# Block 0's partial sums in a fused FNet + MLP layer: residual x copied to DRAM first, block 0 added to it by DMA, and part of the PSUM reads moved from VectorE to ScalarE

## The chip, the cores and the metric

One core of a Trainium2 chip runs the whole layer. The core has TensorE (PE, matrix products into PSUM; its weight loads are listed as PEld), VectorE (DVE), ScalarE (ACT), GpSimd (POOL) and SyncE (SP). SP and POOL also issue DMAs: SP's appear in the profile as queue q1 (hardware_dynamic) and POOL's as q0 (software_dynamic). An adding DMA (`accum_op=ALU.add`) adds its source to what lies at its destination; in this kernel they are all issued by POOL.

The metric is the device time in microseconds of one execution. The kernel before took 1277.23 us, the median of three runs (1274.8 to 1278.28).

## What is computed

With x of 2048 x 576, normalized by rows to xn, the reference is

```python
x = A_x
xn = _layernorm(x, axis=-1)
# A: Real(DFT_seq(DFT_hidden(xn)))
a = jnp.einsum("bsd,ed->bse", xn, dft_hid_re)
b = jnp.einsum("bsd,ed->bse", xn, dft_hid_im)
A = jnp.einsum("ts,bse->bte", dft_seq_re, a) - jnp.einsum("ts,bse->bte", dft_seq_im, b)
# B: an MLP with a hidden width of 4608
h = jnp.maximum(jnp.einsum("bsd,df->bsf", xn, w1), 0)
B = jnp.einsum("bsf,fd->bsd", h, w2)
return x + A + B
```

All inputs are float32. The kernel splits each operand into a float16 high and a float16 low part, and takes three float16 products for one.

## The kernel before

**Stages.** The MLP comes first (up to about 940 us), then the two DFT stages. The MLP's hidden width of 4608 is cut into 9 blocks b of 512 columns, and the 2048 rows of x into 4 groups g of 512 rows (4 tiles of 128). The loop over `steps` (L888) runs over b outside and g inside. A step computes the first product of (b, g) (`mlp1_step` and others, L310 and L335; from b = 2 on `pair_products`, L440), turns it into hidden values h (`mlp1_out`, L343 to L361), and weaves in the second product of the step before, `mlp2` (L496).

**The second product.** `mlp2(b, g, n)` for n = 0 to 6 is one of seven products of a Strassen-like scheme for the four quarters (row, col) of the group's 512 x 576 result. Each is 24 matmuls of 288 columns (L510) into a PSUM tile of the pool `ps2`, which has only two buffers. Products 0, 2, 4 and 6 accumulate in one place, each read out in turn; product 1 has a place of its own, and products 3 and 5 share a third. PE may add the next product to a place only when the one before has been read. The same two buffers are lent to the transposes of x (`transposes`, L254, tiles named pt) and to small products that find a maximum (`power_pe`, L152, tiles named pm).

**Reading a product out.** For b > 0, products 0, 2, 3 and 6 are the first for their quarter: ACT copies them, scaled, into a small buffer (L519). Products 1, 4 and 5 are added to that buffer by DVE (L521), and products 1, 4, 5 and 6 complete a quarter, which POOL then adds to DRAM (`spill`, L523). For b = 0 all seven are added by DVE (L521) into `accs[g]`, the SBUF tile that holds the group's rows of x; after product 6 SP writes the four quarters of `accs[g]` to `spill` by plain DMAs (L527). So `spill` starts as x plus block 0's result, and the other blocks are added to it. At the end of the kernel `load_out` (L1102) reads it back.

**What follows in the place of x.** Once a group's quarters have been written out, `accs[g]` is used again: `sums_x` (L391) forms sums of the transposed xn in float32 (L405 to L409), and writes their high parts (ACT, L412) and low parts (DVE, L414) into the first 2048 of the 2304 floats per partition of `accs[g]`. They are needed from block 2 on. `sums_x` for all groups runs in small steps (`tq`, L887), and the scheduler spreads these over blocks 0 and 1 where it sees room. L414's first write for group 0 lies over parts of the quarters 00 and 01, and so waits for the DMAs that read them.

**Block 0 also normalizes x.** During step (0, g), the tiles of group g + 1 are normalized: statistics (DVE, L200 to L222; ACT, L210), `normalize` (DVE L242, ACT L243), `remainder` (POOL, L247 and L250; its pair of instructions for tile t is called E(t) below) and `transposes` (PE L258 and L263, called T(t) below; ACT L265 and L268 move the result to SBUF).

**Order.** Each engine works through its instructions strictly in order. The order on each engine is fixed when the kernel is built, by a scheduler that follows the program and moves instructions where it expects an engine to be free. POOL and SP issue their DMAs in order too, and one whose data is not ready holds up what stands behind it.

Of the kernel before, what the change touches and what calls it, by code (L numbers as in the profile page):

```python
# [18 lines left out]
P = 128  # L19
# [10 lines left out]
TG = G // P  # L30
# [4 lines left out]
EH = D // 2  # L35
# [14 lines left out]
def kernel(  # L50
# [17 lines left out]
    nc = tc.nc  # L68
# [17 lines left out]
    accs = [accp.tile([P, TG, D], F32, name=f"acc{g}") for g in range(NG)]  # L86
    acc = [accs[t // TG][:, t % TG] for t in range(NT)]

    spill = {
        (g, row, col): dram.tile([P, TG // 2, EH], F32, name=f"spill{g}_{row}{col}")  # L90
        for g in range(NG) for row in range(2) for col in range(2)
    }
    raws = {}

    def load_x(t):
        nc.sync.dma_start(acc[t], x[t * P : (t + 1) * P, :])
# [321 lines left out]
    def pair_products(b, g, i):  # L418
# [70 lines left out]
    places, sums = {}, {(r, j): None for r in range(2) for j in range(2)}  # L489
    turns = itertools.count()  # L490
    sumbufs = [mlp.tile([P, 2, EH], F32, name="sum0", bufs=1)] + [
        dbuf[:, k : k + 2 * EH].rearrange("p (c e) -> p c e", e=EH)
        for k in (2 * W1B, 2 * W1B + 2 * EH)
    ]

    def mlp2(b, g, n):  # L496

        qa, qb, first, row, col = PRODUCTS[n]
        if first:
            places[n] = ps2.tile([P, 2, 512], F32, tag="ps2", name=f"p2_{b}_{g}_{n}")[:, :, :EH]
        ps = places[PLACE[n]]
        for c in range(2):
            for i in range(NQ):
                h, w = hs[b, g, i], w2s[b, i]
                for j, (x, y) in enumerate(((0, 0), (0, 1), (1, 0))):
                    nc.tensor.matmul(  # L510
                        ps[:, c], h[:, x, qa, c * P : (c + 1) * P], w[:, y, qb],
                        start=first and i == 0 and j == 0, stop=i == NQ - 1 and j == 2,
                        skip_group_check=not first,
                    )
        blocks = accs[g].rearrange("p (h c) (j e) -> p h j c e", h=2, j=2)
        o = sums[row, col] = sums[row, col] if b else blocks[:, row, col]
        if b and n in (0, 2, 3, 6):
            o = sums[row, col] = sumbufs[next(turns) % len(sumbufs)]
            nc.scalar.activation(o, ps, AF.Copy, scale=us[b])  # L519
        else:  # L520
            order["acc"] = nc.vector.scalar_tensor_tensor(o, ps, us[b], o, ALU.mult, ALU.add).ins  # L521
        if b and n not in (0, 2, 3):
            nc.gpsimd.dma_start(spill[g, row, col], o, accum_op=ALU.add)  # L523
        if b == 0 and n == 6:
            for r in range(2):
                for j in range(2):
                    nc.sync.dma_start(spill[g, r, j], blocks[:, r, j])  # L527

    sc, pw, mx = {}, {}, {}

# [180 lines left out]
    load_w2(0, 1)  # L711
    for t in range(2 * TG, NT):
        load_x(t)
    warm = const.tile([P, 1], F32, name="warm")
    nc.scalar.activation(warm, eps, AF.Sqrt)

# [91 lines left out]
    for q in range(7):  # L808
        mlp2(0, 0, q)
# [78 lines left out]
    for n in range(2, len(steps)):  # L888
        b, g = steps[n]
# [28 lines left out]
        if b >= BB:  # L918
            first, second = (pair_products(b, g, i) for i in range(NQ))
            later1, later2 = (lambda q, f=f: f(q, True) for f in (first, second))  # L920
            m = lambda q: mlp2(pb, pg, q)
            end = lambda q: ends and ends.pop(0)()
            ready = lambda q: [work() for _ in range(q)]
            count = lambda q: n > 3 and passes and passes.pop(0)()
            for do, q in (
                (first, P1), (first, P2), (m, 0), (end, 0), (first, P6), (ready, 1),
                (first, P5), (later1, P2), (ready, 1), (m, 1), (end, 0), (second, P1), (ready, 1),
                (first, P7), (m, 2), (second, P2), (ready, 1), (first, P3), (first, P4), (count, 0),
                (later1, P7), (m, 3), (second, P6), (later1, P3), (later1, P4), (later2, P2),
                (ready, 1), (m, 4), (second, P5), (ready, 1), (m, 5), (end, 0), (second, P7),  # L930
                (end, 0), (ready, 1), (m, 6), (count, 0), (ready, 2), (second, P3), (second, P4),
                (later2, P7), (later2, P3), (later2, P4), (ready, 1),
            ):
                do(q)
            for _ in range(4):
                next(tq, None)
            continue
        ps = []
        for i in range(NF):
            if n == 2:  # L940
                ps.append(early.pop(0) if early else mlp1(b, g, i))
            else:
                mlp1_step(b, g, i, ps)
            if i % 2:
                mlp1_out(b, g, i // 2, *ps[i - 1 : i + 1])
            if b == 0 and g + 1 < NG:
                t = (g + 1) * TG + i
                normalize(t)
                remainder(t, nc.gpsimd)
                transposes(t)  # L950
            if n == 2 and i == 2:
                todo += prepare_block(1)
            for _ in range(1 if b else 3):
                work()
            for q in range(2 * i, min(2 * i + 2, 7)):
                mlp2(pb, pg, q)
                if b:
                    next(tq, None)
            if b and i == 3:
                next(tq, None)  # L960
            for _ in range(1 + i % 2 if b else 3):
                work()
            if n > 3 and i % 2 and passes:
                passes.pop(0)()
# [146 lines left out]
    for n, (p, kh) in enumerate(units):  # L1111
# [4 lines left out]
        for i, (q, rq, first, row, col) in enumerate(PRODUCTS):  # L1116
# [6 lines left out]
            for k in range(HK):  # L1123
                r = R[kh * HK + k]
# [6 lines left out]
            o = outs[p][:, row, col * EH : (col + 1) * EH]  # L1131
            nc.vector.scalar_tensor_tensor(o, ps, us["c"][:, n : n + 1], o, ALU.mult, ALU.add)  # L1132
            if kh and i in (2, 4, 5, 6):
                h, j = ((0, 0), (1, 1), (0, 1), (1, 0))[(2, 4, 5, 6).index(i)]
                rows = slice((p + h * NP) * P, (p + h * NP + 1) * P)
                e = slice(j * EH, (j + 1) * EH)
# [55 lines left out]
```

## Time and profile before

| | |
|---|---|
| median of three runs | 1277.23 us |
| the profiled execution, whole time | 1277.31 us |
| its span, first to last instruction | 1275.5 us |
| mean granted TensorE clock | 0.999 |
| PE busy | 97% of the span |
| DVE busy | 78% |
| ACT busy | 57% |
| POOL busy | 12% |

Some 1.8 us of the profiled execution lie outside its span. Block 0's second products, which the change touches, run from about 60 us to about 152 us after the span's start. In the prediction, rows with a start, a duration, an engine and a line come from the timeline (instructions in order of time, runs of equal ones merged); in square brackets stands how long the engine had been idle before, and what released it. A matmul's duration in these rows includes its way through the array, so a row of 12 of them that shows 1.63 us is followed by the next after 1.47 us.

### The profile page before, as it was taken

How to read it: one execution, taken by the hardware profiler on the slowest of the kernel's cores; microseconds unless marked ns; L12 is line 12 of the kernel's file. 1: busy time of each engine (PE TensorE's matmuls, PEld its weight loads, DVE VectorE, ACT ScalarE, POOL GpSimd, SP SyncE). 2: the span in 40 equal slices, each digit the busy share in tenths (PEclk: the TensorE clock that was granted, in tenths of full speed). 3: DMA queues.
4: the chain of work that ended last, by engine and by line, in shares of the span. 5: the costliest groups of instructions: out<-in, count | busy, mean ns of one | idle time of the engine just before them, and what ended most of it. 6: DMA issues, size and time to landing. Idle time of an engine off the chain costs nothing.

```text
span 1275.5 us, 25491 instructions
## 1 busy us (share of the span) xinstructions
PE 1242.4 (97%) x10396; PEld 987.9 (77%) x10396; DVE 998.6 (78%) x1875; ACT 730.1 (57%) x1222; POOL 149.2 (12%) x188
## 2 busy tenths in 40 slices
PE   8799999999999999999999999999999999999998
PEld 7565566888888878888888888877777777777776
DVE  8989997786887777777868877546788788878875
ACT  5846466676677676776766766534553333333332
POOL 2320011111112121211111111200000000000000
PEclk9999999999999999999999999999999999999999
DMA  6112457566766575665666665630043434434320
GB/s 244 43 66 66 133 123 151 131 115 146 143 129 126 134 146 126 128 144 120 121 145 142 132 136 120 122 96 1 1 161 104 146 116 153 129 117 143 121 85 20
DMA packets 60806, 150.75 MB, mean 118 GB/s; under 512 B 6288, under 2 KB 21136, under 8 KB 60688
## 3 DMA queue, kind: packets, MB, share of 16 engines
q1 hardware_dynamic: 42256, 111.36, 26.9%
q0 software_dynamic: 18432, 37.76, 20.9%
q8 instruction: 81, 1.33, 0.4%
q14 instruction: 37, 0.30, 0.1%
HBM read 101.91 MB, written 47.19 MB: 117 GB/s over the span
## 4 chain that ended last, share of the span: by engine, by line
PE 62%; DVE 20%; DMA 8%; ACT 6%; issue 4%; POOL 1%; SPq 0%; ACTq 0%; POOLq 0%; DVEq 0%
PE p L1126 23%; PE bank L440 15%; PE p L510 15%; PE pd L1008 7%; DMA raw_w<-in_w_dram 3%; DVE w2s L183 2%; DMA f<-in_cre_dram 1%; PE p L310 1%; DVE h L448 1%; ACT f L880 1%; DVE h L462 1%; ACT h L459 1%; DVE acc L521 1%; DMA spill<-sums 1%; DVE h L354 1%
## 5 line engine op out<-in xcount | busy, mean ns | idle before, releaser
L510 PE MATMUL p<-w2s,h 128*128 128x288 f16 x3024 | 409.7, 286 | 4.4 <-DVE acc L521 2.1
L510 PEld LDWEIGHTS <-h 128*128 128x128 f16 x3024 | 295.1, 98 | 81.5 <-issue 6.2
L1126 PE MATMUL p<-R,cs 128*128 128x288 f16 x2688 | 329.8, 286 | 1.7 <-DVE o L1132 1.7
L1126 PEld LDWEIGHTS <-cs 128*128 128x128 f16 x2688 | 263.0, 98 | 68.3 <-issue 2.0
L182 ACT ACTIVATE cs<-c,sc_c 128x1024 f16<-128x1024 f32 x112 | 128.4, 1148 | 193.2 <-PE p L1126 145.6
L440 PEld LDWEIGHTS <-w1buf 128*128 128x128 f16 x1600 | 156.5, 98 | 29.1 <-issue 8.1
L183 DVE SCALAR_TENSOR_TENSOR cs<-c,sc_c,cs 128x1024 f16<-128x1024 f32 x112 | 143.6, 1282 | 40.8 <-ACT cs L182 40.7
L440 PEld LDWEIGHTS <-dbuf 128*128 128x128 f16 x1200 | 117.4, 98 | 21.4 <-issue 5.8
L440 PE MATMUL bank<-xT,w1buf 128*128 128x256 f16 x832 | 109.9, 273 | 2.7 <-ACT acc L469 2.6
L462 DVE TENSOR_TENSOR h<-s,h 128x1024 f16<-128x1024 f32 x56 | 68.5, 1223 | 48.8 <-ACT h L459 48.8
L440 PE MATMUL bank<-acc,w1buf 128*128 128x256 f16 x768 | 102.1, 272 | 2.8 <-DVE acc L470 1.5
L1008 PE MATMUL pd<-dbuf,xT 128*128 128x288 f16 x832 | 104.1, 286 | 0.6 <-DVE R L1037 0.6
L1008 PEld LDWEIGHTS <-xT 128*128 128x128 f16 x832 | 80.7, 98 | 22.9 <-issue 2.9
L523 POOL DMA_DIRECT2D spill<-dbuf x74 | 64.3, 871 | 289.8 <-DVE dbuf L521 223.3
L440 PE MATMUL bank<-xT,dbuf 128*128 128x256 f16 x624 | 82.3, 273 | 1.4 <-ACT acc L469 1.4
L447 ACT ACTIVATE h<-acc 128x256 f16<-128x256 f32 x112 | 46.3, 414 | 58.8 <-DVE acc L470 42.5
L440 PE MATMUL bank<-acc,dbuf 128*128 128x256 f16 x576 | 76.6, 272 | 2.5 <-DVE acc L470 1.1
L1132 DVE SCALAR_TENSOR_TENSOR o<-p,us_c,o 128x288 f32<-128x288 f32 x112 | 57.4, 512 | 20.1 <-PE p L1126 19.5
L448 DVE SCALAR_TENSOR_TENSOR h<-acc,h 128x256 f16<-128x256 f32 x112 | 47.2, 421 | 32.0 <-ACT h L447 31.8
L459 ACT ACTIVATE h<-s 128x1024 f16<-128x1024 f32 x56 | 59.0, 1053 | 22.5 <-DVE s L454 21.3
L880 ACT ACTIVATE f<-f 128x1024 f32<-128x1024 f32 x64 | 67.2, 1050 | 5.4 <-DMA f<-in_cre_dram 5.4
L519 ACT ACTIVATE dbuf<-p,c_ub 128x576 f32<-128x576 f32 x74 | 54.2, 732 | 20.5 <-ACT h L447 11.3
(161 smaller groups left out, 1531.5 us busy)
## 6 DMA issues: line engine op xcount, KB each, us to landing
spill<-dbuf POOLq DMA_DIRECT2D x74, 288.0 KB, 5.1
f<-in_cre_dram SPq DMA_DIRECT2D x32, 512.0 KB, 4.3
f<-in_cim_dram SPq DMA_DIRECT2D x32, 512.0 KB, 3.8
c<-in_cre_dram SPq DMA_DIRECT2D x32, 512.0 KB, 4.5
c<-in_cim_dram SPq DMA_DIRECT2D x32, 512.0 KB, 4.8
spill<-sum POOLq DMA_DIRECT2D x38, 288.0 KB, 5.1
raw_w<-in_w_dram SPq DMA_DIRECT2D x17, 640.0 KB, 5.0
raw_w<-in_w_dram SPq DMA_DIRECT2D x18, 576.0 KB, 3.8
```

Source lines behind the costliest of these rows:

```text
L182: nc.scalar.activation(hi, src, AF.Copy, scale=s)
L183: nc.vector.scalar_tensor_tensor(lo, src, s, hi, ALU.mult, ALU.subtract)
L440: nc.tensor.matmul(ps, l, r, start=first and m == 0, stop=m == len(todo) - 1, skip_group_check=not first,)
L448: stt(lo, src, 0.0, hi, ALU.max, ALU.subtract)
L459: order["s"] = nc.scalar.activation(hi_s, st[:, 1:], AF.Copy).ins
L462: order["lo"] = nc.vector.tensor_tensor(lo_s, st[:, 1:], hi_s, ALU.subtract).ins
L510: nc.tensor.matmul(ps[:, c], h[:, x, qa, c * P : (c + 1) * P], w[:, y, qb], start=first and i == 0 and j == 0, stop=i == NQ - 1 and j == 2 ...
L523: nc.gpsimd.dma_start(spill[g, row, col], o, accum_op=ALU.add)
L880: nc.scalar.activation(f, f, AF.Abs, scale=2.0**-10, accum_out=sums_c[:, n, q : q + 1])
L1008: nc.tensor.matmul(ps[j], xT[g][:, kx, c * P : (c + 1) * P], dsp[j][:, hl, k], start=(t % 2 == 0 and n == 0), stop=(t % 2 == 1 and n == le ...
L1126: nc.tensor.matmul(ps, w[:, a, k], r[:, c, rq], start=first and k == 0 and j == 0, stop=k == HK - 1 and j == 2, skip_group_check=not first,)
L1132: nc.vector.scalar_tensor_tensor(o, ps, us["c"][:, n : n + 1], o, ALU.mult, ALU.add)
```

## The change

It has three parts.

1. x is copied to `spill` by 16 DMAs from DRAM to DRAM, issued by SP behind the loads of x.
2. Block 0 is treated like the other blocks: products 0, 2, 3 and 6 are copied, scaled, by ACT (the line that was L519), with the quarter of `accs[g]` itself as the target, so that x there is overwritten; products 1, 4 and 5 are added to it by DVE.
3. The finished quarters of block 0 go to `spill` by POOL's adding DMAs (the line that was L523) after products 1, 4, 5 and 6; SP's 16 plain writes (L527) are gone.

```diff
-        blocks = accs[g].rearrange("p (h c) (j e) -> p h j c e", h=2, j=2)
-        o = sums[row, col] = sums[row, col] if b else blocks[:, row, col]
-        if b and n in (0, 2, 3, 6):
-            o = sums[row, col] = sumbufs[next(turns) % len(sumbufs)]
+        if n in (0, 2, 3, 6):
+            if b:
+                o = sumbufs[next(turns) % len(sumbufs)]
+            else:
+                o = accs[g].rearrange("p (h c) (j e) -> p h j c e", h=2, j=2)[:, row, col]
+            sums[row, col] = o
             nc.scalar.activation(o, ps, AF.Copy, scale=us[b])
         else:
+            o = sums[row, col]
             order["acc"] = nc.vector.scalar_tensor_tensor(o, ps, us[b], o, ALU.mult, ALU.add).ins
-        if b and n not in (0, 2, 3):
+        if n not in (0, 2, 3):
             nc.gpsimd.dma_start(spill[g, row, col], o, accum_op=ALU.add)
-        if b == 0 and n == 6:
-            for r in range(2):
-                for j in range(2):
-                    nc.sync.dma_start(spill[g, r, j], blocks[:, r, j])
...
     for t in range(2 * TG, NT):
         load_x(t)
+    for g, row, col in spill:
+        src = x[(g * TG + row * 2) * P : (g * TG + row * 2 + 2) * P, col * EH : (col + 1) * EH]
+        nc.sync.dma_start(spill[g, row, col], src.rearrange("(c p) e -> p c e", p=P))
```

As built, the changed program has the same matmuls. On POOL, the adding DMA for group 0's quarter 00 stands ahead of E(12) to E(15), the next 12 adding DMAs stand behind E(15), and POOL's two reductions (L121) for block 2's weights come after 13 of the 16. DVE's order around block 0 is also different, since the scheduler fills the room that 16 instructions leave.

## The prediction

> **What bounds the kernel now.** I read the page first (busy shares, then the slices), then the busy time by stretches, then the waits of PE up to 200 us, and at last the timeline from 56 to 152 us, where block 0's second products run.
>
> ```profile
> span 1275.5 us, 25491 instructions
> PE 1242.4 (97%) x10396; PEld 987.9 (77%) x10396; DVE 998.6 (78%) x1875; ACT 730.1 (57%) x1222; POOL 149.2 (12%) x188
> ```
>
> PE is the bound: 97% of the span. The change leaves PE's work as it is, so it can only move the time PE waits. The stretches (length; PE, PEld, DVE, ACT, POOL busy with counts; clock; DMA share; GB/s) tell where that is:
>
> ```profile
> 60.00:80.00 20.00, 18.43 (x126) 11.85 (x126) 18.34 (x42) 9.43 (x16) 6.90 (x8) 1.00 0.26 83
> 80.00:100.00 20.00, 18.47 (x142) 12.39 (x142) 14.73 (x30) 9.42 (x16) 0.00 (x0) 1.00 0.18 61
> 160.00:180.00 20.00, 20.00 (x128) 11.99 (x127) 19.93 (x36) 14.41 (x26) 4.08 (x5) 1.00 0.62 140
> ```
>
> From 160 us PE has no gap, though DVE is as full: DVE relief is worth nothing there. From 60 to 100 us PE misses 3.1 us. The waits of PE up to 200 us (total, times, longest) name the part that is due to L521:
>
> ```profile
> PE p L510 <- DVE acc L521: 2.1, 5, 0.6
> PE pm L158 <- DVE acc L521: 0.9, 1, 0.9
> ```
>
> That is 3.0 us in six waits. A gap hides up to 0.16 us of a matmul's tail (12 matmuls show 1.63 us, the next start 1.47 us later), so at most 3.0 + 6 x 0.16 = 4.0 us can be won.
>
> **Amounts.**
>
> ```profile
> L242 DVE TENSOR_SCALAR dbuf<-acc,mv,r 128x576 f32<-128x576 f32 x4 | 2.7, 716 | 0.0
> L521 DVE SCALAR_TENSOR_TENSOR acc<-p,c_ub,acc x28: 800/808/819, 67.9 to 148.5; 128x576 f32<-128x576 f32 x28
> L519 ACT ACTIVATE dbuf<-p,c_ub 128x576 f32<-128x576 f32 x74 | 54.2, 732 | 20.5 <-ACT h L447 11.3
> L523 POOL DMA_DIRECT2D spill<-dbuf x18: 856/865/1032, 165.6 to 299.7; - x18
> spill<-dbuf POOLq DMA_DIRECT2D x74, 288.0 KB, 5.1
> spill<-acc SPq DMA_DIRECT2D x16, 288.0 KB, 2.6
> L523 POOL DMA_DIRECT2D spill<-sum x9: 860/865/1213, 154.7 to 287.7; - x9
> DMA to landing us min/median/max: 2.5/4.4/6.1
> ```
>
> Sixteen of the 28 L521 go (16 x 0.808 = 12.9 us of DVE) and sixteen ACT copies come (16 x 0.732 = 11.7 us); ACT was 47% busy there and has room, but its order matters. A quarter written by SP was in DRAM 2.6 us after its issue; one added by POOL takes 5.1 us, after 0.87 us of POOL each (16 x 0.87 = 13.9 us of a POOL that is busy 6.9 us in 40). The last row is the range of landings of both kinds up to 300 us. What counts is who waits for a landing.
>
> **Copies of x and SP's queue.**
>
> ```profile
> 2.11 0.91 SPq L96 DMA_DIRECT2D acc<-in_x_dram  x2
> L527 SPq DMA_DIRECT2D spill<-acc x16: 513/513/626, 70.4 to 149.3; - x16
> 17.98 0.33 SPq L873 DMA_DIRECT2D f<-in_cre_dram  x1
> 57.09 2.06 SPq L107 DMA_DIRECT2D raw_w<-in_w_dram  x2
> DMA packets 1273, 3.22 MB, mean 403 GB/s; under 512 B 141, under 2 KB 141, under 8 KB 1271
> DMA packets 4, 0.06 MB, mean 2 GB/s; under 512 B 0, under 2 KB 0, under 8 KB 0
> ```
>
> The last two rows are the DMA totals for 9 to 17 us and 24 to 57 us. The copies are 16 x 0.295 = 4.7 MB, issued where f stood, at 18 us. At 403 GB/s they take 12 us, at half that 23 us, and end by about 47 us in a gap where almost nothing else moves. The next load, raw_w at 57.09, waited for its buffer, not for SP, and keeps its time; cover gone (under 140 GB/s), it and ACT's L581 behind it would slip. The first adding DMA needs its copy only at 70 us. I take 0, bounds 0 and 2 us. SP's sixteen writes vanish; the weight loads behind them waited for their buffers too: 0.
>
> **The path that sets the end: group 0, 66 to 88 us.**
>
> ```profile
> 67.91 0.30 ACT L210 ACTIVATE u<-mv,eps 128x4 f32<-128x4 f32 x1 [1.85 <-DVE mb L587]
> 67.94 0.82 DVE L521 SCALAR_TENSOR_TENSOR acc<-p,c_ub,acc 128x576 f32<-128x576 f32 x1
> 68.67 0.17 DVE L211 RECIPROCAL r<-u 128x4 f32<-128x4 f32 x1
> 69.55 0.81 DVE L521 SCALAR_TENSOR_TENSOR acc<-p,c_ub,acc 128x576 f32<-128x576 f32 x1
> 71.46 0.31 POOL L247 TENSOR_TENSOR dbuf<-dbuf 128x64 f16<-128x64 f32 x1 [22.36 <-DVE dbuf L242]
> 73.33 1.38 POOL L250 TENSOR_TENSOR dbuf<-dbuf 128x512 f16<-128x512 f32 x1
> 74.74 0.78 DVE L405 TENSOR_TENSOR dbuf<-xT 128x512 f32<-128x512 f16 x1 [0.32 <-POOL dbuf L250]
> 77.00 0.81 DVE L521 SCALAR_TENSOR_TENSOR acc<-p,c_ub,acc 128x576 f32<-128x576 f32 x1
> 77.20 1.16 POOL L250 TENSOR_TENSOR dbuf<-dbuf 128x512 f16<-128x512 f32 x1
> 82.18 0.69 DVE L414 TENSOR_TENSOR acc<-dbuf,acc 128x512 f16<-128x512 f32 x1 [0.63 <-DMA spill<-acc]
> 82.79 0.81 DVE L521 SCALAR_TENSOR_TENSOR acc<-p,c_ub,acc 128x576 f32<-128x576 f32 x1
> 83.85 0.81 DVE L521 SCALAR_TENSOR_TENSOR acc<-p,c_ub,acc 128x576 f32<-128x576 f32 x1
> 84.71 0.66 PE L258 MATMUL pt<-ident,dbuf 128*128 128x128 f16 x9
> 85.06 1.23 DVE L361 TENSOR_TENSOR h<-s,h 128x1024 f16<-128x1024 f32 x1 [0.40 <-ACT h L360]
> 86.20 0.81 DVE L521 SCALAR_TENSOR_TENSOR acc<-p,c_ub,acc 128x576 f32<-128x576 f32 x1
> ```
>
> T(13) at 84.71 starts when L521 for group 1's product 1 ends (83.85 + 0.81): it takes that product's PSUM buffer. That L521 came after L414, which already waited 0.63 us for the plain write of quarter 01. In the changed order DVE runs L414, then L361, then this L521, then T(13) may start. So:
>
> 1. ACT copies product 0 at about 67.95 to 68.68 and only then runs L210 (0.30). DVE's small steps ahead of product 1's L521 began at 68.67 and that L521 at 69.55, 0.88 later; they now begin at 69.0, and the L521 ends at 70.7 (before 70.36).
> 2. POOL issues quarter 00 at 70.75. Its price for the new shape (two runs of 1152 bytes per partition, not one of 2304) is not in the trace: bounds 0.87 and twice that, 1.74. SP's issues of that shape took 0.513 us against 0.455 for loads of x with long runs, 1.13 times. I take 1.2 times, 1.06, since the near row is of SP, not of POOL. E(12) starts at 71.85 (before 71.46); E(12) to E(15) took 71.46 to 78.36 = 6.9 us, so POOL is free at 78.75. Quarter 11 takes it to 79.81, when quarter 01 is issued. Landing 5.1 us later: 84.9. Bounds for the landing: 2.6 (the plain write) and 6.1 (the longest).
> 3. DVE arrives at L414 earlier: L405 must wait for E(13) as at 74.74 (now 75.1), then L406, product 4's L521, L409 and product 5's L521 at some 0.75 each bring it to 78.6 (that L521 ended at 77.81 before), and six reads of the first product to about 81.6. It waits 3.3 us.
> 4. After the landing: L414 0.61 (82.18 to 82.79), L361 1.14 (85.06 to 86.20), L521 0.81 and 0.05 to PE: 2.6 us. T(13) at 87.5, against 84.71: +2.8. The new PE order puts two more L510 matmuls (2 x 0.12) ahead of T(13): **+2.55**.
>
> PE stands still meanwhile, since everything in its order is behind T(13). T(12) slips too, to 78.7 (77.86 before), inside this sum.
>
> On POOL's issue the trace and a rule disagree. The 27 issues above stayed within 856 and 1213 ns, some of them in a stretch with DVE busy 19.93 of 20 us. The Trainium skill ("SBUF — State Buffer", "Who interferes with whom") says that VectorE in a two-port mode, which tensor_scalar can enter, locks GpSimd out whole. Quarter 00 would then be issued only behind the four L242. The sum without this is +2.55; with it, see the second rival.
>
> **The rest of block 0.** Five rows of the timeline:
>
> ```profile
> 99.67 0.22 PE L158 MATMUL pm<-ident,mb 128*1 128x128 bf16 x1 [0.91 <-DVE acc L521]
> 119.58 0.68 DVE L414 TENSOR_TENSOR acc<-dbuf,acc 128x512 f16<-128x512 f32 x1
> 133.82 0.42 PE L510 MATMUL p<-w2s,h 128*128 128x288 f16 x2 [0.45 <-ACT h L360]
> 132.95 0.38 POOL L121 PARTITION_ALL_REDUCE top<-c_mw  x1 [54.59 <-ACT w1buf L581]
> 143.77 0.14 DVE L124 TENSOR_SCALAR half<-top 128x1 f32<-128x1 f32 x1
> ```
>
> Group 1's last quarter was complete at 99.6 (pm waited for it), its first L414 came at 119.58: 20 us in which its adding DMAs land, so no wait. ACT's copy of product 6 stands behind L360 and L182, but PE has the next first product to do: 0. The wait of pm for L521 (0.91 us) becomes one for ACT's L268 behind an L182; I price it equal. The hidden values of group 3 held PE for 0.45 us at 133.82; the new order calls for them sooner and DVE is earlier: 0, bounds -1 and +1.
>
> L121, now behind 13 adding DMAs, has 10 us until DVE reads it, and DVE's copy of L124 stands 22 instructions behind the L521 that the thirteenth needs: 0. Beyond 152 us PE is full: 0.
>
> Sum: 1277.31 + 2.55 = **1279.8 us**, +0.2% on the median of 1277.23. A difference below 0.3% (3.8 us) is about what a measurement of this kernel can't tell from no change.
>
> **Rivals.**
>
> *Relief wins.* DVE has 12.9 us less, and if quarter 01 lands before DVE reaches L414, the six waits on L521 go: 1277.31 - 4.0 = 1273.3. For it: DVE is 92% busy from 60 to 80 us. Against it: the order on POOL puts 6.9 us of E ahead of quarter 01, and ACT's copies stand behind waits of their own. Chance 0.12.
>
> *Slower.* The place is the same wait at L414, and a landing after 86.2 us decides: each microsecond later is one more at T(13). POOL held up until the four L242 behind product 1's L521 end, at 70.9 + 4 x 0.72 = 73.8, gives E(12) at 74.0, E(15) done 80.9, quarter 01 issued 82.0 and landed 87.1: T(13) at 89.7, +4.8 net, 1282.1. An issue of 1.74 us and a landing of 6.1 give 72.5, 79.4, 81.1, 87.2: the same. For it: E's own L250 took 1.38 us at 73.33, 1.16 at 77.20, so POOL is slowed there. Against it: no L523 beyond 1.21 us. Chance 0.36.
>
> *No new wait of weight.* Adding lands as fast as writing, 2.6 us: 82.4, T(13) at 85.0, +0.1 net, 1277.4. Against it stand 74 DMAs at 5.1. The Trainium skill ("DMA: Bandwidth & Descriptors", "Anatomy of one DMA — SWDGE (gpsimd) path") would give it: 2.0 us plus bytes over 436 GB/s, an estimate of 2.7 us for this size; the measured 5.1 decides. Chance 0.10.
>
> *The copies are late*: +2 at most, 1281.8. Chance 0.04.
>
> **How the numbers follow.** My case (+1.5 to +3.8, a landing between 83.9 and 86.2 us) has 0.38. Range: from 1275.3 (half the relief) to 1284.1 (the slower rival at 1282.1 with one unknown of +2 on top). Mine and "no new wait" lie within 0.3%: same 0.48; slower 0.40; faster 0.12.
>
> **What would show it.** DVE idle some 3 us before group 0's first L414, released by a spill DMA; T(13) near 87.5 and PE idle before it by about 2 us; POOL's issue of quarter 01 after E(15), near 80; copies of x done before 57 us; PE without gaps beyond 152 us. If L414 waits under 1 us, or a PE gap of over 1 us shows up elsewhere in 90 to 152 us, the prediction is wrong.

## The result, and the profile after

The changed kernel took 1282.74 us (median; 1282.27 to 1283.88), the kernel before, run beside it, 1277.24 us. The ratio is 1.0045, 95% interval 1.0032 to 1.0059: some 5.7 us slower, at least 4.1.

Of the page of the changed kernel, the span and the busy row:

```profile
span 1281.0 us, 25506 instructions
PE 1242.9 (97%) x10396; PEld 988.9 (77%) x10396; DVE 989.9 (77%) x1859; ACT 739.8 (58%) x1238; POOL 165.5 (13%) x204
```

VectorE lost 8.7 us of work and PE's work is the same, but the span grew by 5.5 us (1275.5 before). The busy time by stretches of the changed kernel (length; PE, PEld, DVE, ACT, POOL; clock; DMA share; GB/s) says where:

```profile
60.00:80.00 20.00, 15.21 (x100) 9.74 (x100) 15.00 (x36) 9.60 (x16) 7.74 (x9) 1.00 0.27 60
80.00:100.00 20.00, 18.90 (x137) 12.98 (x137) 9.28 (x17) 10.35 (x17) 6.50 (x6) 0.91 0.52 64
100.00:120.00 20.00, 17.09 (x109) 9.22 (x108) 18.10 (x40) 14.04 (x25) 2.18 (x2) 1.00 0.61 114
160.00:180.00 20.00, 20.00 (x127) 12.33 (x126) 19.93 (x41) 11.89 (x21) 3.43 (x4) 1.00 0.62 140
```

From 60 to 80 us PE misses 4.8 us (1.6 before), from 100 to 120 us 2.9 us (none before); from 160 us it is full, as before. From 60 to 100 us VectorE is far from full (24.3 of 40 us, 33.1 before) and PE waits more all the same. That points to the order of the instructions and not to VectorE's capacity; the experiments test it. PE's waits up to 400 us (total, times, longest), those that grew by 0.5 us or more:

```profile
PE p L510 <- DVE acc L524: 4.4, 1, 4.4
PE pm L158 <- DVE mb L619: 1.8, 1, 1.8
PE p L310 <- ACT xT L265: 1.5, 2, 1.2
PE pt L258 <- DVE acc L524: 1.0, 1, 1.0
```

L524 is the add that was L521, L526 GpSimd's DMA that was L523, L521 now ScalarE's copy. The first wait is the largest. To find the products in the rows: the traces have 3024 L510 matmuls for 252 second products, 12 for each (not 24), so product 6 of group 0 is the row of 12 at 80.00. Timeline of the changed kernel around group 0, VectorE's rows, then GpSimd's, then PE's:

```profile
70.79 2.04 DVE L242 TENSOR_SCALAR dbuf<-acc,mv,r 128x576 f32<-128x576 f32 x4
75.50 1.92 DVE L405 TENSOR_TENSOR dbuf<-xT 128x512 f32<-128x512 f16 x1 [2.66 <-POOL dbuf L250]
77.45 1.77 DVE L406 TENSOR_TENSOR dbuf<-dbuf,xT 128x512 f32<-128x512 f32 x1
79.14 0.81 DVE L524 SCALAR_TENSOR_TENSOR acc<-p,c_ub,acc 128x576 f32<-128x576 f32 x1
...
80.47 0.81 DVE L524 SCALAR_TENSOR_TENSOR acc<-p,c_ub,acc 128x576 f32<-128x576 f32 x1
...
87.31 0.69 DVE L414 TENSOR_TENSOR acc<-dbuf,acc 128x512 f16<-128x512 f32 x1 [2.90 <-DMA spill<-acc]
87.92 1.22 DVE L361 TENSOR_TENSOR h<-s,h 128x1024 f16<-128x1024 f32 x1
89.05 0.81 DVE L524 SCALAR_TENSOR_TENSOR acc<-p,c_ub,acc 128x576 f32<-128x576 f32 x1
...
70.93 1.53 POOL L526 DMA_DIRECT2D spill<-acc  x1 [21.60 <-DVE sh L222]
...
74.07 1.39 POOL L250 TENSOR_TENSOR dbuf<-dbuf 128x512 f16<-128x512 f32 x1
...
75.46 1.37 POOL L250 TENSOR_TENSOR dbuf<-dbuf 128x512 f16<-128x512 f32 x1
...
76.83 1.83 POOL L250 TENSOR_TENSOR dbuf<-dbuf 128x512 f16<-128x512 f32 x1
80.26 1.11 POOL L526 DMA_DIRECT2D spill<-acc  x1 [1.60 <-DVE acc L524]
81.58 1.08 POOL L526 DMA_DIRECT2D spill<-acc  x1 [0.21 <-issue]
...
80.00 2.19 PE L510 MATMUL p<-w2s,h 128*128 128x288 f16 x12 [4.40 <-DVE acc L524]
81.99 1.16 PE L258 MATMUL pt<-ident,dbuf 128*128 128x128 f16 x9
...
89.92 0.66 PE L258 MATMUL pt<-ident,dbuf 128*128 128x128 f16 x9 [1.03 <-DVE acc L524]
```

Read it from L405. With four of group 0's instructions moved to ScalarE, the scheduler put L405 and L406 ahead of product 4's add. In the kernel before, that add stood between them (L405 is the row at 74.74) and ended at 76.25:

```profile
75.44 0.81 DVE L521 SCALAR_TENSOR_TENSOR acc<-p,c_ub,acc 128x576 f32<-128x576 f32 x1
76.16 0.91 DVE L406 TENSOR_TENSOR dbuf<-dbuf,xT 128x512 f32<-128x512 f32 x1
```

Now VectorE idles 2.66 us in L405 until E(13) is done (the L250 at 74.07), L405 and L406 take 1.92 and 1.77 us beside GpSimd's E(14) and E(15) (0.78 and 0.91 before), and product 4's add ends at 79.95. PE's product 6 (80.00) accumulates on that place and stands 4.40 us. Product 5's add is late with it and ends at 81.28; quarter 01 is complete only then, is issued at 81.58, and L414, which waits until it has landed, starts at 87.31, 5.7 us later. T(13) follows L414, L361 and the add: 89.92 (84.71 before).

The third loss is at 119 us (SyncE, ScalarE, PE of the same timeline):

```profile
108.51 3.91 SPq L100 DMA_DIRECT2D raw_w<-in_w_dram  x2
...
113.84 1.16 ACT L609 ACTIVATE j<-raw_w 128x1152 f32<-128x1152 f32 x1 [2.42 <-DMA raw_w<-in_w_dram]
...
119.03 0.27 PE L158 MATMUL pm<-ident,mb 128*1 128x128 bf16 x2 [1.76 <-DVE mb L619]
```

ScalarE sits in L609 until block 1's w2 has landed, 5.3 us after its issue; its L353, VectorE's L354 behind that, the small L619 behind both and PE's pm wait in turn.

### The profile page after: what moved, and what is told of

It is laid out like the page before. It is cut to its first block, busy times and chain, and to the rows that moved or that the text cites. A ratio compares the mean times of both kernels' runs of the same rounds, so it can differ in the third digit from the quotient of the medians.

```text
span 1281.0 us, 25506 instructions
## 1 busy us (share of the span) xinstructions
PE 1242.9 (97%) x10396; PEld 988.9 (77%) x10396; DVE 989.9 (77%) x1859; ACT 739.8 (58%) x1238; POOL 165.5 (13%) x204
## 4 chain that ended last, share of the span: by engine, by line
PE 70%; DVE 11%; DMA 6%; ACT 5%; issue 2%; POOL 1%; SPq 0%; POOLq 0%; ACTq 0%; DVEq 0%
PE p L1128 25%; PE p L510 18%; PE bank L440 16%; PE pd L1010 7%; PE p L310 4%; DMA raw_w<-in_w_dram 2%; DVE w2s L183 2%; DMA f<-in_cre_dram 1%; ACT f L882 1%; ACT h L459 1%; DVE h L462 1%; DVE h L448 1%; DMA c<-in_cre_dram 1%; DMA spill<-sums 1%; ACT j L609 1%
## 5 line engine op out<-in xcount | busy, mean ns | idle before, releaser
L510 PE MATMUL p<-w2s,h 128*128 128x288 f16 x3024 | 409.3, 286 | 6.8 <-DVE acc L524 4.4
L510 PEld LDWEIGHTS <-h 128*128 128x128 f16 x3024 | 295.6, 98 | 82.9 <-issue 8.3
L526 POOL DMA_DIRECT2D spill<-dbuf x74 | 64.1, 869 | 291.0 <-DVE dbuf L524 225.1
L521 ACT ACTIVATE dbuf<-p,c_ub 128x576 f32<-128x576 f32 x74 | 54.1, 733 | 19.2 <-ACT h L447 11.2
```

Of the source, the lines that this page charges most:

```text
L510: nc.tensor.matmul(ps[:, c], h[:, x, qa, c * P : (c + 1) * P], w[:, y, qb], start=first and i == 0 and j == 0, stop=i == NQ - 1 and j == 2 ...
```

## The experiments

Two theories stood at the start. **A, order:** product 4's add stands behind L405, which waits for GpSimd and runs slowly beside it. **B, landing:** the prediction's, T(13) waits for quarter 01. A third, **C**, says that the adding DMAs cost by themselves. Below, *held* means that `sums_x` of group 0 may start only behind a given add.

Single profiles differ in how soon the first second product starts (58.9 to 62.1 us), whatever the kernel. So each trace is measured from one mark, the first seven L510 that wait for ScalarE's L268. In the kernel before and in the changed one:

```profile
60.17 1.02 PE L510 MATMUL p<-w2s,h 128*128 128x288 f16 x7 [1.24 <-ACT xT L268]
```

```profile
60.39 1.02 PE L510 MATMUL p<-w2s,h 128*128 128x288 f16 x7 [1.24 <-ACT xT L268]
```

The ratio tells the cost in time, the two distances tell where it arises: T(12) and T(13) are the first L258 rows behind group 0's product 6 and inside group 1's products.

| | ratio to before, 95% interval | T(12), us after the mark | T(13) |
|---|---|---|---|
| before | | 17.69 | 24.54 |
| changed | 1.0045 (1.0032 to 1.0059) | 21.60 | 29.53 |
| e1 product 4's add ahead of L405 | 1.0037 (1.0022 to 1.0052) | 19.62 | 26.72 |
| e2 plain writes | 1.0020 (1.0011 to 1.0030) | 20.78 | 26.08 |
| e3 copies by VectorE | 1.0045 (1.0031 to 1.0059) | 19.98 | 28.22 |
| e4 sums_x held for long | 1.0004 (0.9996 to 1.0013) | 16.52 | 22.37 |
| e5 sums_x held shortly | 0.9991 (0.9980 to 1.0001) | 16.52 | 22.37 |
| e6 before, held for long | 0.9987 (0.9977 to 0.9996) | 17.23 | 23.81 |
| e7 before, copies of x added | 1.0006 (0.9992 to 1.0021) | 17.69 | 24.80 |
| e8 adding DMAs behind E | 1.0054 (1.0037 to 1.0070) | 20.78 | 30.36 |
| e9 groups 1 to 3 changed | 1.0001 (0.9992 to 1.0010) | 17.69 | 23.94 |
| e10 the same, held shortly | 0.9997 (0.9987 to 1.0006) | 17.24 | 22.77 |
| e11 before, held shortly | 0.9989 (0.9979 to 0.9998) | 17.24 | 23.82 |
| e12 plain writes, held shortly | 0.9988 (0.9976 to 1.0000) | 16.52 | 22.38 |

### e1: product 4's add first

```diff
             order["acc"] = nc.vector.scalar_tensor_tensor(o, ps, us[b], o, ALU.mult, ALU.add).ins
+            if b == 0:
+                order["add", g, n] = order["acc"]
...
     def sums_x(g):
+        held = [order["add", 0, 4]] if g == 0 else []
...
-            if tail:
+            if held:
+                h2, l2 = halves(g, tail)
+                with tc.issue_after(held.pop()):
+                    tt(t, h, h2, ALU.subtract)
+                    tt(t, t, l2, ALU.subtract)
+            elif tail:
```

> The changed kernel (1282.74 us) with one difference on VectorE: the first steps of sums_x for group 0 (L405, L406) are held behind the add of group 0's product 4, which stood behind them. Theory A (order): the 4.40 us for which TensorE waits ahead of product 6 are VectorE sitting in L405, which waits for GpSimd's E(13) (75.46 us) and, beside E(14) and E(15), runs 1.92 us and L406 1.77 us where 0.68 us is usual. With the add first it runs at about 75.7, when product 4 ends, and that wait falls from 4.4 to under 1 us. Theory B (the prediction's: the landing): quarter 01 is still issued behind E(15), at about 80, and lands near 85.5, so group 0's first L414 ends near 86.2 and T(13) starts at about 87.0, not 89.9. Both together: 2.9 us less, 1279.8. If only A counts (T(13) does not wait), 1278.8; if the adding DMAs cost by themselves, as a third theory has it, no change: 1282.7.

The line numbers behind the edit are higher, in e1, e4 and e5 alike: L407 and L408 are L405 and L406, L420 is L414, L530 the add. Timeline of e1, PE and VectorE:

```profile
79.95 0.66 PE L258 MATMUL pt<-ident,dbuf 128*128 128x128 f16 x9 [2.94 <-DVE acc L530]
87.05 0.66 PE L258 MATMUL pt<-ident,dbuf 128*128 128x128 f16 x9 [1.82 <-DVE acc L530]
...
75.43 1.92 DVE L407 TENSOR_TENSOR dbuf<-xT 128x512 f32<-128x512 f16 x1 [0.43 <-POOL dbuf L250]
...
85.58 0.69 DVE L420 TENSOR_TENSOR acc<-dbuf,acc 128x512 f16<-128x512 f32 x1 [2.71 <-DMA spill<-acc]
```

The add came at 74.19 and product 6 did not wait. A place that the expectation had not counted took over: product 5's add still stood behind L407 and L408, and T(12) waited 2.94 us for it. Quarter 01 landed at 85.58 and T(13) came at 87.05: theory B at the size expected (87.0). So both exist, and each hides behind the other.

In the traces the gain is there. Quarter 01 lands 1.7 us sooner than in the changed kernel, and the add for T(13) stands ahead of L361. PE's 0.34 us wait for L354 comes 72.3 us after the mark (74.9 in the changed kernel). The times show less of it: 2.9 us below the changed kernel was expected, and 1.0037 against 1.0045, some 1 us with overlapping intervals, can't be told from no gain.

### e2: plain writes instead of the adding DMAs

```diff
-        if n not in (0, 2, 3):
+        if b and n not in (0, 2, 3):
             nc.gpsimd.dma_start(spill[g, row, col], o, accum_op=ALU.add)
+        if b == 0 and n == 6:
+            for r in range(2):
+                for j in range(2):
+                    nc.sync.dma_start(spill[g, r, j], sums[r, j])
```

> The changed kernel with SyncE's four plain writes per group after product 6, as before the change, in place of GpSimd's adding DMAs of block 0; ScalarE's copies, VectorE's order (L405 and L406 ahead of product 4's add) and the copies of x stay. The plain writes overwrite the copied x, so x is missing from the result. GpSimd has no DMA ahead of E(12): E(13) ends about 1.1 us sooner. Theory A (order): the wait ahead of product 6 stays at about 3.3 us, the wait at L414 is short, 1280.6. Theory C (GpSimd's DMAs are the whole of the loss): both waits go, and the time is at most that of before, 1274 to 1277.

The wait ahead of product 6 stayed, at 2.77 us, and T(13) did not wait for a landing: order costs without a single adding DMA in block 0. C is not the whole. 1.0020 (some 2.6 us above the kernel before) lies between the kernels, a little better than A alone had it (1280.6).

### e3: the copies by VectorE

```diff
-            nc.scalar.activation(o, ps, AF.Copy, scale=us[b])
+            if b:
+                nc.scalar.activation(o, ps, AF.Copy, scale=us[b])
+            else:
+                nc.vector.tensor_scalar(o, ps, us[b], None, ALU.mult)
```

> The changed kernel with block 0's copies of products 0, 2, 3 and 6 done by VectorE, so that VectorE has its work of before; the copies of x and the adding DMAs stay. VectorE's order is then close to that before: product 4's add stands between L405 and L406. Theory A (order): the wait ahead of product 6 is under 2 us. Theory B (landing) alone is left: T(13) waits for L414 as in the prediction's sum, +2 to +3 on before, 1279.5 to 1280.5. If the adding DMAs do all the harm, 1282.7 or more, since VectorE has 12.9 us more to do than in the changed kernel.

The wait ahead of product 6 fell to 0.19 us, as order has it. The time was a miss: two L242 took 3.67 us beside GpSimd (1.63 us before) and held up product 3's copy behind them, for which PE waited 2.68 us; then group 1's first copy stood behind the L414 that waits for the landing (PE 2.43 us). So handing the copies back to VectorE does not bring the time back, and this run does not test order alone; the wait at L414 holds up whatever is queued behind it.

### e4 and e5: sums_x of group 0 out of the way

Against e1:

```diff
-        held = [order["add", 0, 4]] if g == 0 else []
+        held = [order["add", 1, 5]] if g == 0 else []
```

> The changed kernel with sums_x for group 0 held back until group 1's product 5 has been added (about 20 us later): neither L405 nor L414 stands between group 0's products and T(13), so both theory A's wait (4.4 to under 1) and theory B's (1.03 to 0) go, and with the standstill the lower clock granted after it (0.83 from 80 to 90 us): 1276 to 1278.5. The rival: VectorE, 98% busy or more from 100 to 120 us before the change, gets the same work later and gives the gain back there: 1280 or more.

For e5 the add is `order["add", 1, 1]`, the one that frees T(13)'s buffer.

> The changed kernel with sums_x for group 0 held only until group 1's product 1 has been added, the add that frees T(13)'s buffer (about 82 us). Group 0's products, T(12) and T(13) then go as where the steps were held for 20 us: product 6 and T(12) without a wait, T(13) at about 82.9, not 89.9. But sums_x is not crowded into the time from 100 to 160 us as much, so of the 3.5 us for which TensorE waited there for ScalarE's copies some go. If L405 and L414 in group 0's window are the whole of the loss and the crowding is what was given back: 1274 to 1276 on a chip where the kernel before has 1275.9, and the changed kernel some 1281.4. Rival: the late waits come from ScalarE's copies standing behind its waits for weight loads whatever sums_x does: about 1276.4, as with the longer hold.

Timeline of e4, PE:

```profile
77.06 0.67 PE L258 MATMUL pt<-ident,dbuf 128*128 128x128 f16 x9
82.91 0.66 PE L258 MATMUL pt<-ident,dbuf 128*128 128x128 f16 x9
```

Both without a wait, and in both variants T(13) is 7.2 us sooner after the mark than in the changed kernel and 2.2 us sooner than before. That is the relief the prediction's first rival had in mind (the 2.1 us of waits on L521 are gone). With the long hold the time is that of before (1.0004), and PE has new gaps later: ScalarE waits for block 2's weights, and its copies behind that wait keep PE (1.06 us at 137.85 us). With the short hold those copies do not wait, and the largest late gap is 1.69 us at 110.83 us (below, with e12).

### e6 and e11: the same holds in the kernel before

> A control: the kernel before, unchanged but for sums_x of group 0 held back until group 1's product 5 has been added. If the hold is a gain of its own, this is faster than before by 1 us or more, and the changed kernel with the hold then is a loss against it; if the hold only repairs what the change broke, this is within 0.5 us of before or slower. In the kernel before, TensorE waited 2.1 us for the adds (L521) in that window; L405 and L406 (1.7 us of VectorE) stand between those, so a gain of 0 to 1 us is expected, given back later where VectorE is full: within 1 us of before.

> The kernel before with the shorter hold (sums_x of group 0 until group 1's product 1 has been added), the same hold as in the best variant of the changed kernel. If the change is worth something once sums_x is out of the way, this one is slower than the changed kernel with the same hold by 1 us or more; if the change is neutral then, the two are within 0.7 us: 1275 to 1276 where before is 1277.

The edits are those of e4 and e5. The expected gain from the hold alone was 0 to 1 us, given back; measured 1.7 us (0.5 to 2.9) and 1.4 us (0.3 to 2.7). L405, L406 and L414 were in the way in the kernel before too, only less. With the short hold the times agree, changed or not: 0.9991 (e5) and 0.9989 (e11). With the long hold they do not: 1.0004 (e4) against 0.9987 (e6), some 2.2 us in disfavour of the change, with intervals that only touch at 0.9996. The two held versions of the kernel before are the only ones whose interval lies below both kernels.

### e7: copies of x alone

The diff is the change's first part (the copies of x) alone, put into the kernel before.

> The kernel before with the 16 copies of x to DRAM added and nothing else (the plain writes then overwrite them): the copies are over by about 45 us and the next load waits for its buffer until 57 us, so no difference from before, within 0.5 us. Rival: DMA traffic of 0.91 of the engines from 20 to 40 us delays something: +1 to +2 us.

No difference that can be measured (0.9992 to 1.0021, so up to 2.7 us is not ruled out), and T(12) at the same distance.

### e8: group 0's adding DMAs behind E(12) to E(15)

```diff
-            nc.gpsimd.dma_start(spill[g, row, col], o, accum_op=ALU.add)
+            add = lambda: nc.gpsimd.dma_start(spill[g, row, col], o, accum_op=ALU.add)
+            if b == 0 and g == 0:
+                pending.append(add)
+            else:
+                add()
...
-        eng.tensor_tensor(
+        order["rem"] = eng.tensor_tensor(
             xs[:, D + REM :], xn[:, : KM * P], xs[:, : KM * P], ALU.subtract
-        )
+        ).ins
...
                 remainder(t, nc.gpsimd)
+                if i == 3 and pending:
+                    with tc.issue_after(order["rem"]):
+                        for add in pending:
+                            add()
+                    pending.clear()
```

> The changed kernel with group 0's adding DMAs behind E(12) to E(15) on GpSimd, VectorE's order unchanged. E(13) ends about 1.1 us sooner (74.3), so L405 starts at 74.4 and product 4's add ends near 78.8: the wait ahead of product 6 falls from 4.4 to about 3.3. Quarter 01 is issued third of three DMAs, at about 81, and lands near 86.5, so T(13) is hardly sooner (89.3). 0.5 to 1.1 us less than the changed kernel. If GpSimd's issue ahead of E, not VectorE's order, were what costs, most of the 5.5 us would come back.

A miss: 0.5 to 1.1 us less than the changed kernel was expected, and 1.0054 came, no gain and perhaps a loss (the intervals overlap). Product 4's add did end sooner (78.26) and the wait ahead of product 6 fell to 2.77 us. But quarter 00 was now issued at 78.75 and not at 70.93, and something nobody had waited for became late. Timeline of e8, VectorE, ScalarE, PE:

```profile
75.19 0.78 DVE L405 TENSOR_TENSOR dbuf<-xT 128x512 f32<-128x512 f16 x1 [2.43 <-POOL dbuf L250]
76.00 1.52 DVE L406 TENSOR_TENSOR dbuf<-dbuf,xT 128x512 f32<-128x512 f32 x1
...
85.69 0.63 ACT L412 ACTIVATE acc<-dbuf 128x512 f16<-128x512 f32 x1 [2.34 <-DMA spill<-acc]
...
87.95 2.56 PE L512 MATMUL p<-w2s,h 128*128 128x288 f16 x10 [2.32 <-ACT acc L523]
```

ScalarE's L412 writes over quarter 00, waits for its landing, and the copies behind it keep PE for 2.32 us.

### e9, e10 and e12: what is left outside group 0

e9 leaves group 0 as it was before the change; e10 adds the short hold.

```diff
+        blocks = accs[g].rearrange("p (h c) (j e) -> p h j c e", h=2, j=2)
+        old = b == 0 and g == 0
+        if old:
+            sums[row, col] = blocks[:, row, col]
-        if n in (0, 2, 3, 6):
+        if n in (0, 2, 3, 6) and not old:
...
+        if old and n == 6:
+            for r in range(2):
+                for j in range(2):
+                    nc.sync.dma_start(spill[g, r, j], blocks[:, r, j])
-        if n not in (0, 2, 3):
+        if n not in (0, 2, 3) and not old:
             nc.gpsimd.dma_start(spill[g, row, col], o, accum_op=ALU.add)
...
     for g, row, col in spill:
+        if g == 0:
+            continue
```

> The changed kernel with group 0 as before the change (all seven products added by VectorE into x in place, four plain writes, no copy of its x); groups 1 to 3 as changed. If the loss sits in group 0's window, where sums_x starts, T(13) starts at about 85, as before the change (84.71), and not at 89.92, and the time is that of before plus at most the 1.8 us for which TensorE waits near 119 us: 1277 to 1279. If adding DMAs or ScalarE's copies cost in every group, three quarters of the 5.5 us stay: 1281.

> The same (group 0 as before the change, groups 1 to 3 as changed), with sums_x of group 0 held until group 1's product 1 has been added. Hold and mix should both keep group 0's window clear, so nothing is added by the second: within 1 us of the changed kernel with the hold alone (0.999 of before), 1275 to 1277. If the adds on VectorE in group 0's window still cost TensorE their 2 us, it is slower than that by up to 2 us.

With group 0 alone put back, the whole loss is gone (1.0001). Three changed groups of four cost nothing, on balance, that can be measured: T(13) is 0.6 us sooner than before, and 1.66 us at 112 us go the other way. The 5.7 us hang on group 0. e12 is e2 with the short hold.

> SyncE's plain writes in place of block 0's adding DMAs (x is missing from the result), ScalarE's copies, and the same hold: the relief of VectorE by itself, with neither of the two costs. Against the changed kernel with the hold (0.999 of before) it saves what the adding DMAs cost there: the 1.7 us for which TensorE waits near 111 us behind a late load of weights should fall to about 0.5, as with plain writes without the hold. So 1.2 us less, 0.998 of before. If adding DMAs cost nothing beyond group 0's window: no difference.

e5 and e12 agree up to T(13) and issue block 1's w2 at the same distance from the mark (40.96 and 40.97 us). ScalarE's wait for it, in e5 and then in e12:

```profile
105.65 1.16 ACT L617 ACTIVATE j<-raw_w 128x1152 f32<-128x1152 f32 x1 [2.35 <-DMA raw_w<-in_w_dram]
```

```profile
105.37 1.16 ACT L621 ACTIVATE j<-raw_w 128x1152 f32<-128x1152 f32 x1 [1.07 <-DMA raw_w<-in_w_dram]
```

The load landed 5.26 us after its issue with block 0's adding DMAs, 3.98 us with plain writes; PE's wait at pm was 1.69 and 0.41 us. Without the hold the pair is the same: 5.3 and 4.0 us, 1.76 and 0.46 us in the changed kernel and in e2. So the adding DMAs cost some 1.3 us there: in the traces C is real, and small. In the time (0.9991 and 0.9988) the intervals do not tell e5 and e12 apart.

## Why the prediction came out as it did

The place was right (group 0, the wait of L414 for quarter 01, T(13) behind it), the size was not: +2.55 us was forecast and about +5.7 us came. The largest wait, 4.40 us ahead of product 6, is nowhere in the sum. By the prediction's own line of 0.3% the result is "slower", to which it gave 0.40, and not "same", which it held likeliest at 0.48. That the time lies near the slower rival's price (1282.1), and so inside the range, is in part luck, since that rival had another reason.

*ScalarE ahead of L210, GpSimd's issue.* E(12) started at 72.05 us (forecast 71.85), E(15) ended at 78.66 (78.75), an undisturbed issue took 1.08 us (1.06). Right. Quarter 00's took 1.53 us beside the L242; it was not locked out until they ended, which the slower rival had assumed.

*Quarter 01 behind E(15), near 80.* Wrong. E(15) was done at 78.66, but quarter 11 waited for product 4's add and was issued at 80.26, and 01 came behind both that issue (81.37) and product 5's add (81.28), at 81.58. **The step that failed is the third:** "L406, product 4's L521, L409 and product 5's L521 at some 0.75 each bring it to 78.6". L405 and L406 alone took 3.7 us, and product 5's add ended at 81.28, not near 78.6. The list named the adds, in the right order, but never asked who waits for product 4's (PE's product 6) and product 5's (quarter 01). So T(12), put at 78.7, came at 81.99.

*Landing 5.1 us.* 5.7 us, inside its bounds. The issue 1.8 us and the landing 0.6 us late make the 2.4 us between the 87.5 us forecast for T(13) and 89.92. L414's wait was 2.90 us (3.3 forecast), PE's ahead of T(13) 1.03 us (2 forecast): PE had already stood for 4.40 us and then worked at a lower clock (last section). e1, in which product 6 does not wait, puts T(13) 2.2 us behind before.

*The rival "slower"* gave a landing at 87.1 us and T(13) at 89.7 us for a GpSimd held by L242. Its numbers came true (87.31, 89.92) by another way, so by luck: it was VectorE that was held by GpSimd.

*The rest of block 0: 0.* The wait of pm priced as equal fell on the L310 ahead of pm and was 1.15 us at 104.89 for 0.91 us before: nearly right. The 1.76 us at 119 us were missed; by the prediction's own test, a gap of over 1 us there, it was wrong on that. The load behind it was issued 48.1 us after the mark, 6.5 us later than before (41.6), and 5.0 us of that is the shift of T(13). But the shift is not the reason for the wait: e5 issues the load at 40.96 and still has 1.69 us of it. With plain writes 0.4 to 0.5 us of it are left; the rest is the slower landing beside adding DMAs, a term that the sum did not have. The gaps of 0.17, 0.45 and 0.19 us near 130 us in the kernel before shrank to one of 0.34 us.

*Copies of x: 0.* No run speaks against it (e7: 1.0006). *Relief: up to 4.0 us where nothing new is waited for.* 2.2 us of it showed at T(13) in e4, e5 and e12.

*What stays open.* Whether the changed kernel with the short hold is better or worse than the kernel before with it can't be told from these runs; with the long hold it was some 2.2 us worse, and PE's waits for ScalarE's copies (1.06 us at 137.85 and 0.74 us at 161.28 in e4) are gaps that e6 does not have. Orders with the adds of both products 4 and 5 ahead of L405, and no hold beyond that, were not tried.

## What to carry to other kernels

When work leaves an engine, read the new order of what stays: an instruction that waits for another engine, moved ahead of a PSUM read, can cost more than the work saved: here VectorE had 8.7 us less to do and the kernel took 5.7 us more. For each instruction behind a wait ask who needs it, and hold the one that nobody needs yet: here holding back steps whose results are needed from block 2 on removed the whole loss. Then give the same hold to the kernel before as well: it gained 1.4 to 1.7 us, and nothing of the change's own gain was left to see. A read moved to another engine also joins that engine's waits for loads and landings.

## What the runs showed of the hardware

**VectorE and GpSimd slow each other, by kind of operand.** L405 and L406, with both inputs in SBUF, took 0.68 us alone and 1.92 and 1.77 us beside GpSimd's L250. GpSimd lost where VectorE had started first: its L250 took 1.60 us behind L405 at 74.93 in the kernel before and 1.16 us at 77.20. The add, with one input in PSUM, took 0.81 us beside GpSimd's L250 (77.00 in the kernel before) and 0.81 us without it (79.14 in the changed kernel). The Trainium skill ("SBUF — State Buffer", "Who interferes with whom") says just this: a VectorE instruction with two SBUF inputs contends with a GpSimd instruction that reads SBUF, one with at most one such input and outside the two-port modes does not. The trace agrees, and the prediction had taken from that section only the locking out of GpSimd. One tensor input in SBUF is not safe by itself: two L242 took 1.06 us with GpSimd idle (70.35 in the kernel before), and 1.63 us and, in e3, 3.67 us beside it.

**A standstill of PE can halve its clock for about 3.4 us** (an estimate from the mean of 0.83 over the 10 us from 80 to 90 us in the changed kernel: half the clock for 3.4 us). Stretches of 1 us of the changed kernel, of e2 and of e1, each shortly behind a wait (the clock is the third number from the end):

```profile
81.00:82.00 1.00, 1.00 (x7) 0.59 (x5) 0.35 (x2) 0.70 (x3) 0.79 (x2) 0.50 0.18 8
```

```profile
78.00:79.00 1.00, 1.00 (x6) 0.61 (x4) 1.00 (x2) 0.55 (x1) 0.00 (x0) 0.50 0.43 158
```

```profile
81.00:82.00 1.00, 1.00 (x9) 0.72 (x8) 1.00 (x3) 1.00 (x3) 1.00 (x2) 1.00 0.95 136
```

The clock was 0.50 behind waits of 4.40 us and 2.77 us (in e8 also, behind its 2.77 us, 0.50 from 79 to 80 us), and full behind one of 2.94 us in e1, so the length of the wait alone does not decide. The Trainium skill ("TensorE: Matmul & The Clock Gate", "Part 1: The HAM clock gate (the "warmup" mystery)") puts the drop behind an idle window of about 3.4 us that runs freely; here 2.77 us was enough, in two runs. In the changed kernel T(13) waited for the landing even so (1.03 us), so the half clock did not delay it; in e2, where T(13) did not wait, nothing hid it.

**An adding DMA keeps the DMA engines busier.** DMA totals from 60 to 100 us, by queue (packets, MB, share of the 16 engines' time), of the kernel before (plain writes, with some 0.45 MB of other loads) and of the changed one (adding):

```profile
q1 hardware_dynamic: 2081, 2.81, 20.9%
```

```profile
q0 software_dynamic: 1438, 1.56, 31.8%
```

That is 7.4% per MB against 20.4%, 2.7 times as much.
